# Windowed attention in blocks of 32 queries by 64 keys: scores and value products as 64x32 tiles of the TensorE array

## The chip, the cores and the metric

The kernel runs on one core of a Trainium2 chip. The metric is device time in microseconds (us): the median of three runs. One further execution was recorded by the profiler; its rows are what the text below quotes. PE is TensorE (matmuls), PEld its weight loads, DVE VectorE, ACT ScalarE, POOL GpSimd, SP the engine that issues most DMAs. PSUM is the memory that matmuls write, in banks of 2 KB a partition.

## The reference

Attention over 8 batches, 8 heads, 576 tokens and head size 64, with a window: the first four heads see the last 32 positions, the other four every fourth of the last 128. Behind it a rank-32 mix along the sequence (U, V) and a feed-forward layer of 512 to 2048 to 512.

```python
scores = scale * np.matmul(q, k.transpose(0, 1, 3, 2))
mask_plain = (rel >= 0) & (rel < window)                       # window 32
mask_dil = (rel >= 0) & (rel < window * dilation) & (rel % dilation == 0)
scores = np.where(masks, scores, -1000000000.0)
attn = np.exp(scores - max);  attn = attn / (sum + 1e-09);  a = attn @ v
x = a.transpose(0, 2, 1, 3).reshape(B, S, H * D)
h = x.transpose(0, 2, 1) @ U @ V
u = x + h.transpose(0, 2, 1)
out = u + np.maximum(u @ w_ch1, 0.0) @ w_ch2
```

## The kernel before

**Layout.** The host permutes the tokens of the dilated heads so that they too see 32 successive rows. A tile is 64 queries of one half of the heads, and it needs 64 + 32 = 96 keys. A group is two such tiles for the four heads of a half, taken as two pairs (u, h); a batch has nine groups, the kernel 72. What a group computes is masked: of 96 keys a query uses 32.

**A step of attention.** `batch_items` makes eleven steps a batch. Step s first issues the products with v of group s-2 (`products`, L386), then the scores of group s (`scores`, L337), then the division by the sum (`weighted`, L393 to L417); the sum is a column of ones in v, so that v has 65 columns a head. `soften` follows in four pieces: DVE adds the mask and takes the maximum in one operation (L347), ACT takes the exponential (L351). `turn` brings the result to keys by queries: for the first 18 groups by four PE transposes (L361), behind them by eight DVE transposes of 32x32 blocks (L371). Steps 0 and 1 of a batch have scores alone, the last two products alone.

**A matmul's place in the array.** The scores have 64 contraction rows and 64 queries, so that four tiles of 64x64 lie in the array of 128x128. The products have 96 rows and 64 queries, two tiles.

**The mix.** `split` cuts x in a high and a low part (ACT L440, DVE or POOL L442), `t_mm` multiplies by U (L473; five parts of the batch, some with 64 rows, two matmuls each), `t_evict` splits the result (L482 to L486), `mix` multiplies by V (L495) and DVE adds it to x (L497). `turn_x` turns x by DVE transposes and DRAM, `transp` by PE (L548); ACT L553 and DVE L554 make its high and low part (uth, utl).

**The layers.** 36 tiles of 128 tokens go in twelve chunks of three. For each of 16 f of a chunk layer 1 is twelve matmuls of 128x384 into a PSUM tile ph (L714: high w by high u, low by high, high by low), ACT writes hh, DVE hl (L720), and layer 2 is nine matmuls of 128x512 (L734). The three acc tiles are added to x at the end (L759).

**What sets the order.** Attention of batch 0 is the prologue. The work of the other batches is cut into a queue with due times in chunks, 1.5 chunks a batch, and `slot()` puts what is due between the matmuls of the layers. From chunk 1 on PE's order is that of the code (`tc.manual_schedule(engines={PE})`, PE_FROM = 1); in the prologue, in chunk 0, and on the other engines a scheduler sets it. In the prologue and chunk 0 the weights are read and split in a high and a low part as well (L194 to L210).

**PSUM.** Eight banks: "acc" with three, "ph" with two, "ps" with three. "ps" is shared by the products and half of the scores (`banks`), the other half of the scores (s), the four transposes (ptp) of batch 1, the U products (t), the V products (m) and the transposed tiles (tp). In batch 0 scores use "acc" and transposes "ph".

## Time and profile before

| | us |
|---|---|
| three runs: median (lowest to highest) | 1002.73 (999.86 to 1003.53) |
| the profiled execution | 1000.64 |
| its span in the trace | 998.9 |
| first layer-1 matmul of chunk 0 / of chunk 1 | 52.49 / 152.30 |
| PE busy | 973.3, 97% |
| mean granted clock of TensorE | 0.998 |

The chain that ended last, by line, starts so:

```profile
PE ph L714 37%; PE acc L734 37%; PE b L386 4%; PE s L337 3%; PE t L473 2%; DMA v<-vv 1%; ACT p L351 1%; ACT sign L195 1%; ACT sign L196 1%; ACT v L194 1%; DMA raw<-w 1%; PE m L495 1%; DVE utl L554 1%; DMA raw<-vt 1%; PE t L462 1%
```

Three quarters of the time are matmuls of the two layers; the attention's own matmuls are 7% of it. A matmul row of the timeline gives start and length in us, the line, output and inputs, the contraction rows by columns held (96*64), the columns streamed (96x65) and the number of records that follow one another (x16); a fp32 matmul has two records. Layer matmuls are one record each. "f32" stands for fp32r as well.

### The profile page before, as it was taken

How to read it: one execution, taken by the hardware profiler on the slowest of the kernel's cores; microseconds unless marked ns; L12 is line 12 of the kernel's file. 1: busy time of each engine (PE TensorE's matmuls, PEld its weight loads, DVE VectorE, ACT ScalarE, POOL GpSimd, SP SyncE). 2: the span in 40 equal slices, each digit the busy share in tenths (PEclk: the TensorE clock that was granted, in tenths of full speed). 3: DMA queues.
4: the chain of work that ended last, by engine and by line, in shares of the span. 5: the costliest groups of instructions: out<-in, count | busy, mean ns of one | idle time of the engine just before them, and what ended most of it. 6: DMA issues, size and time to landing. Idle time of an engine off the chain costs nothing.

```text
span 998.9 us, 17702 instructions
## 1 busy us (share of the span) xinstructions
PE 973.3 (97%) x6696; PEld 834.6 (84%) x6696; DVE 512.7 (51%) x1704; ACT 320.2 (32%) x785; POOL 134.4 (13%) x136
## 2 busy tenths in 40 slices
PE   6899999999999999999999999999999999999998
PEld 4687777888888898888888888888888888899897
DVE  2579887654367435664357634664536743211211
ACT  4699963222224212232123312232222421111110
POOL 1289850011001100011000200001100110000000
PEclk9999999999999999999999999999999999999999
DMA  9678624321224122341223313342222303100000
GB/s 276 186 231 273 216 67 130 101 85 59 73 77 124 47 75 67 93 119 48 75 61 100 94 28 77 95 127 60 70 62 79 100 17 95 44 1 1 32 1 32
DMA packets 74805, 89.78 MB, mean 90 GB/s; under 512 B 8256, under 2 KB 53376, under 8 KB 74720
## 3 DMA queue, kind: packets, MB, share of 16 engines
q1 hardware_dynamic: 74720, 88.65, 30.5%
q8 instruction: 53, 0.87, 0.4%
q14 instruction: 32, 0.26, 0.1%
...
## 4 chain that ended last, share of the span: by engine, by line
PE 85%; ACT 5%; DMA 4%; DVE 3%; issue 1%; POOL 1%; SPq 0%; DVEq 0%; ACTq 0%
PE ph L714 37%; PE acc L734 37%; PE b L386 4%; PE s L337 3%; PE t L473 2%; DMA v<-vv 1%; ACT p L351 1%; ACT sign L195 1%; ACT sign L196 1%; ACT v L194 1%; DMA raw<-w 1%; PE m L495 1%; DVE utl L554 1%; DMA raw<-vt 1%; PE t L462 1%
## 5 line engine op out<-in xcount | busy, mean ns | idle before, releaser
L734 PE MATMUL acc<-w2h,hh 128*128 128x512 f32 x576 | 231.1, 401 | 0.3 <-ACT hh L719 0.3
L734 PE MATMUL acc<-w2h,hl 128*128 128x512 f32 x576 | 225.9, 398 | 4.5 <-DVE hl L720 4.4
L734 PE MATMUL acc<-w2l,hh 128*128 128x512 f32 x576 | 227.0, 394 | 0.0
L720 DVE SCALAR_TENSOR_TENSOR hl<-ph,hh 128x384 fp32r<-128x384 f32 x192 | 106.3, 555 | 234.7 <-ACT hh L719 233.4
L719 ACT ACTIVATE hh<-ph 128x384 fp32r<-128x384 f32 x192 | 93.8, 489 | 404.4 <-PE ph L714 403.8
L714 PE MATMUL ph<-uth,w1h 128*128 128x384 f32 x768 | 169.1, 341 | 0.9 <-ACT uth L553 0.9
L714 PE MATMUL ph<-utl,w1h 128*128 128x384 f32 x768 | 167.3, 338 | 0.8 <-DVE utl L554 0.8
L714 PE MATMUL ph<-uth,w1l 128*128 128x384 f32 x768 | 167.2, 338 | 0.0
L714 PEld LDWEIGHTS ph<-uth,w1h 128*128 128x128 f32 x768 | 136.8, 188 | 16.3 <-ACT uth L553 1.2
L371 DVE STREAM_TRANSPOSE pt<-p 32x128 f32<-32x128 f32 x432 | 130.4, 302 | 27.2 <-ACT p L351 21.7
L351 ACT ACTIVATE p<-p,nmax 128x96 f32<-128x96 f32 x288 | 91.3, 367 | 164.0 <-DVE nmax L347 160.5
L714 PEld LDWEIGHTS ph<-utl,w1h 128*128 128x128 f32 x768 | 134.2, 188 | 3.3 <-DVE utl L554 1.1
L734 PEld LDWEIGHTS acc<-w2h,hl 128*128 128x128 f32 x576 | 107.7, 187 | 34.7 <-DVE hl L720 9.5
L714 PEld LDWEIGHTS ph<-uth,w1l 128*128 128x128 f32 x768 | 134.4, 188 | 2.1 <-issue 0.6
L442 POOL TENSOR_TENSOR xhl<-x,xhl 128x256 fp32r<-128x256 f32 (+1 forms) x65 | 50.3, 781 | 627.0 <-ACT xhl L440 603.3
L734 PEld LDWEIGHTS acc<-w2h,hh 128*128 128x128 f32 x576 | 107.9, 187 | 20.7 <-issue 1.1
L734 PEld LDWEIGHTS acc<-w2l,hh 128*128 128x128 f32 x576 | 108.2, 188 | 15.5
L347 DVE CUSTOM_DVE_ANT_0 p<-s,mask_sb 128x96 f32<-128x96 f32 x162 | 34.6, 253 | 82.3 <-PE b L337 69.3
L386 PEld LDWEIGHTS b<-v,pt 96*64 96x64 f32 x1152 | 41.7, 143 | 21.5 <-issue 18.7
L337 PE MATMUL s<-qk 64*64 64x96 f32 x648 | 47.3, 280 | 8.1 <-DMA qk<-qk 6.5
L497 DVE TENSOR_TENSOR x<-x,m 128x256 f32<-128x256 f32 (+1 forms) x74 | 30.5, 416 | 46.9 <-PE m L495 41.7
L386 PE MATMUL b<-v,pt 96*64 96x65 f32 x1152 | 52.2, 234 | 0.0
...
## 6 DMA issues: line engine op xcount, KB each, us to landing
...
v<-vv SPq DMA_DIRECT2D x126, 97.5 KB, 2.0
...
```

Of the source, the lines that this page charges most:

```text
L337: nc.tensor.matmul(sp[h][i * QB:(i + 1) * QB, u, :], lhsT=q_, rhs=k_, start=True, stop=True, tile_position=(h * D, i * QB))
L347: nc.vector.tensor_tensor_reduce(out=p_sb[:, n], in0=sp[h][:, u], in1=mask_sb[:, mask_kind(*tile_of(g, 0))], scale=-1.0 / 8.0, scalar=3.0e ...
L351: nc.scalar.activation(out=p_sb[:, n], in_=p_sb[:, n], func=AF.Exp, bias=nmax[:, n:n + 1], scale=-1.0,)
L371: nc.vector.transpose(out=pt[ks, :, rs], in_=p_sb[rs, :, ks])
L386: last_pv[g] = nc.tensor.matmul(pv[rows[i]:rows[i] + QB, 2 * u + h, :], lhsT=pt[:, 2 * u + h, QB * i:QB * (i + 1)], rhs=loaded[g, 1, i][:, ...
L442: eng.tensor_tensor(out=xl[rs], in0=x[rs], in1=xh[rs].bitcast(F32), op=ALU.subtract)
L473: nc.tensor.matmul(t_ps[b, c], lhsT=u[rs], rhs=m[rs], start=(i == 0 and k == 0), stop=(i == len(batch_parts(b)) - 1 and k == 1),)
L497: nc.vector.tensor_tensor(out=x, in0=x, in1=mp[rs], op=ALU.add)
L714: nc.tensor.matmul(ph, lhsT=w[:, k, :], rhs=u[:, k, :], start=(n == 0), stop=(n == len(seq) - 1))
L719: nc.scalar.activation(out=hh, in_=ph, func=AF.Relu)
L720: nc.vector.scalar_tensor_tensor(out=hl, in0=ph, scalar=0.0, in1=hh.bitcast(F32), op0=ALU.max, op1=ALU.subtract)
L734: nc.tensor.matmul(acc[i], lhsT=h[:, ss], rhs=w, start=(c > 0 and f == 0 and n == 0), stop=(f == FC - 1 and n == 2))
```

## The change

Queries go in blocks of 32, and each block needs 64 keys. A group of two tiles has four blocks (r) and its scores are 16 matmuls of 64 contraction rows by 32 queries with 64 keys, for eight tiles of the array. The products contract over the 64 keys of a block, again 16 matmuls of 64 rows by 32 queries with 65 columns; the two u lie on the upper and the lower half of the rows. Scores and products of a step write one PSUM tile of two banks ("att", one buffer); the even groups of batch 0 use two "acc" banks instead. "ps" keeps one buffer of its three, for everything else in it. The mask, the maximum, the subtraction and the exponential are done for the whole group: two additions of 128 columns, a maximum, a subtraction over 256 columns, one exponential of 256. A group has two PE transposes of 128x128 in place of four, or sixteen DVE transposes of 32 by 2x32 in place of eight of 32 by 4x32. v is loaded with 128 rows in place of 96, with the overlapping keys twice. Parts of the U products that have 64 rows are brought to 128: POOL clears the other rows. Lines of the layers move to L727, L732 to L733 and L747, of the V products to L508, of the final addition to L772.

```diff
-KB = QB + WIN
+KT = QB + WIN
+KB = 2 * WIN
...
-    psum = ctx.enter_context(tc.tile_pool(name="psum", bufs=3, space=bass.MemoryType.PSUM))
+    psum = ctx.enter_context(tc.tile_pool(name="psum", bufs=1, space=bass.MemoryType.PSUM))
...
-    def banks(name):
-        t = psum.tile([P, UNITS * DV + 2 * KB], F32, tag="ps", name=name)
-        return (t[:, 0:UNITS * DV].rearrange("p (u e) -> p u e", e=DV),
-                t[:, UNITS * DV:].rearrange("p (u k) -> p u k", k=KB))
+    def banks(g):
+        if g >= NGB or g % 2:
+            t = psum.tile([P, 2, 512], F32, tag="att", name=f"att{g}", bufs=1)
+            return [t], [t[:, 0], t[:, 1]]
+        t = [psum.tile([P, 512], F32, tag="acc", name=f"att{g}_{i}", bufs=3) for i in range(2)]
+        return [e.unsqueeze(1) for e in t], t
...
-                for i in range(2):
-                    q_, k_ = q_and_k(g, u, h, i)
-                    nc.tensor.matmul(sp[h][i * QB:(i + 1) * QB, u, :], lhsT=q_, rhs=k_, start=True, stop=True,
-                                     tile_position=(h * D, i * QB))
+                for r in range(BLK):
+                    q_, k_ = q_and_k(g, u, h, r)
+                    nc.tensor.matmul(each[h][r * WIN:(r + 1) * WIN, u * KB:(u + 1) * KB], lhsT=q_, rhs=k_,
+                                     start=True, stop=True, tile_position=(h * D, r * WIN))
...
-        nc.vector.tensor_tensor_reduce(
-            out=p_sb[:, n], in0=sp[h][:, u], in1=mask_sb[:, mask_kind(*tile_of(g, 0))], scale=-1.0 / 8.0, scalar=3.0e38,
-            op0=ALU.add, op1=ALU.min, accum_out=nmax[:, n:n + 1],
-        )
-        nc.scalar.activation(
-            out=p_sb[:, n], in_=p_sb[:, n], func=AF.Exp,
-            bias=nmax[:, n:n + 1], scale=-1.0,
-        )
+                nc.vector.tensor_tensor(out=o, in0=e[:, h, 0:2 * KB].rearrange("p (u k) -> p u k", k=KB),
+                                        in1=m.broadcast_to([P, 2, KB]), op=ALU.add)
+        p4 = p_sb.rearrange("p h u k -> p (h u) k")
+        nc.vector.tensor_reduce(out=top, in_=p4, axis=mybir.AxisListType.X, op=ALU.max)
+        nc.vector.tensor_tensor(out=p4, in0=p4, in1=top.unsqueeze(2).broadcast_to([P, UNITS, KB]), op=ALU.subtract)
+        nc.scalar.activation(out=p4, in_=p4, func=AF.Exp, scale=1.0 / 8.0)
...
-        for r in range(P // WIN):
+        for r in range(BLK):
             rs = slice(WIN * r, WIN * (r + 1))
-            for k in (r % 2, r % 2 + 1):
-                ks = slice(WIN * k, WIN * (k + 1))
-                nc.vector.transpose(out=pt[ks, :, rs], in_=p_sb[rs, :, ks])
+            for u in range(2):
+                for k in range(2):
+                    ks = slice(D * u + WIN * k, D * u + WIN * (k + 1))
+                    nc.vector.transpose(out=pt[ks, :, rs], in_=p_sb[rs, :, u, WIN * k:WIN * (k + 1)])
...
-                for i in range(2):
-                    last_pv[g] = nc.tensor.matmul(pv[rows[i]:rows[i] + QB, 2 * u + h, :], lhsT=pt[:, 2 * u + h, QB * i:QB * (i + 1)],
-                                     rhs=loaded[g, 1, i][:, u, hs], start=True, stop=True)
+                for r in range(BLK):
+                    row = rows[r // 2] + r % 2 * WIN
+                    o = 2 * KB + h * DV
+                    last_pv[g] = nc.tensor.matmul(each[u][row:row + WIN, o:o + DV], lhsT=pt[us_, h, WIN * r:WIN * (r + 1)],
+                                                  rhs=loaded[g, 1, r // 2][us_, r % 2, hs], start=True, stop=True,
+                                                  tile_position=(u * D, row))
...
+        if rs != slice(0, P):
+            rest = slice(0, rs.start) if rs.start else slice(rs.stop, P)
+            nc.gpsimd.memset(xhl[rest].bitcast(F32), 0.0)
...
-                t_ps[b, c], lhsT=u[rs], rhs=m[rs],
+                t_ps[b, c], lhsT=u, rhs=m,
...
-        mp = psum.tile([P, HALF_D], F32, tag="ps", name=f"m{b}_{i}_{c}")
+        mp = psum.tile([P, HALF_D], F32, tag="ps", name=f"m{b}_{i}_{c}", bufs=1)
...
-            tp = psum.tile([P, KC, P], F32, tag="ps", name=f"tp{t}")
+            tp = psum.tile([P, KC, P], F32, tag="ps", name=f"tp{t}", bufs=1)
```

What it moves, in three places. PE, a full step of batch 2's kind in chunk 1, before (the last products of one group, the scores of another, and the layer matmul behind them; b and s are PSUM tiles of "ps"):

```order
L386 MATMUL b_4_2235<-v_0_2148,pt_79 64x65
L386 MATMUL b_4_2235<-v_1_2150,pt_79 64x65
L386 MATMUL b_4_2235<-v_0_2148,pt_79 64x65
L386 MATMUL b_4_2235<-v_1_2150,pt_79 64x65
L337 MATMUL s_2244<-qk_2080 64x96 x2
L337 MATMUL b_4_2235<-qk_2080 64x96 x2
L337 MATMUL s_2244<-qk_2080 64x96 x2
L337 MATMUL b_4_2235<-qk_2080 64x96 x2
L714 MATMUL ph_5_2263<-uth_1919,w1h_86 128x384 x4
```

and the same step after:

```order
L387 MATMUL att_2483<-v_0_2376,pt_79 32x65 x2
L387 MATMUL att_2483<-v_1_2378,pt_79 32x65 x2
L387 MATMUL att_2483<-v_0_2376,pt_79 32x65 x2
L387 MATMUL att_2483<-v_1_2378,pt_79 32x65 x2
L333 MATMUL att_2483<-qk_2302 32x64 x16
L727 MATMUL ph_5_2525<-uth_2107,w1h_84 128x384 x4
```

The step stands where it stood; it has 16 and 16 matmuls in place of 8 and 8, into one tile.

PE, the passage from chunk 0 to chunk 1, before (acc is the last of layer 2, m are V products of batch 1, tp tiles turned by PE, ph the first of layer 1):

```order
L734 MATMUL acc_2_687<-w2h_1537,hl_15_1916 128x512
L495 MATMUL m_3_0_1715<-ts_0_1675,vs 128x256
L495 MATMUL m_4_0_1721<-ts_0_1675,vs 128x256
L337 MATMUL s_1875<-qk_1153 64x96 x4
L337 MATMUL b_0_1874<-qk_1153 64x96 x4
L548 MATMUL tp_1921<-id_sb,x_399 128x128 x4
L548 MATMUL tp_1928<-id_sb,x_389 128x128 x4
L548 MATMUL tp_1952<-id_sb,x_1096 128x128 x4
L714 MATMUL ph_0_1979<-uth_1919,w1h_86 128x384 x4
```

and after, from the third U product on (two more stand ahead of it, behind the last of layer 2):

```order
L486 MATMUL t_0_1790<-xhl_3_0_1809,us 64x256 x2
L486 MATMUL t_0_1790<-xhl_4_0_1840,us 64x256 x2
L508 MATMUL m_0_0_1867<-ts_0_1859,vs 128x256
L508 MATMUL m_1_0_1879<-ts_0_1859,vs 128x256
L508 MATMUL m_2_0_1890<-ts_0_1859,vs 128x256
L508 MATMUL m_3_0_1899<-ts_0_1859,vs 128x256
L508 MATMUL m_4_0_1905<-ts_0_1859,vs 128x256
L561 MATMUL tp_2109<-id_sb,x_461 128x128 x4
L561 MATMUL tp_2116<-id_sb,x_449 128x128 x4
L561 MATMUL tp_2148<-id_sb,x_1248 128x128 x4
L727 MATMUL ph_0_2175<-uth_2107,w1h_84 128x384 x4
```

The U products and the first three V products, which lay among the last layers of chunk 0, stand between the chunks now; the scores have left that place.

DVE, one group in the steady part, before (ssum and xp are the division of an older group, p the softmax, pt its transposes, hl the remainder of layer 1):

```order
L393 TENSOR_SCALAR ssum_4525<-b_2_4503 128x4
L394 RECIPROCAL ssum_4525<-ssum_4525 128x4
L417 TENSOR_TENSOR xp_4528<-b_2_4503,ssum_4525 128x256
L347 ISA p_4521,nmax_4522<-b_2_4503,mask_sb 128x96
L347 ISA nmax_4522 128x1
L347 ISA p_4521,nmax_4522<-b_2_4503,mask_sb 128x96
L347 ISA nmax_4522 128x1
L371 STREAM_TRANSPOSE pt_79<-p_4521 32x4x32 x8
L720 SCALAR_TENSOR_TENSOR hl_2_4550<-ph_2_4532,hh_2_4549 128x384
```

and one after (this group's division writes two x tiles of 64 rows):

```order
L398 TENSOR_SCALAR ssum_4278<-att_4242 128x4
L400 RECIPROCAL ssum_4278<-ssum_4278 128x4
L425 TENSOR_TENSOR x_2734<-att_4242,ssum_4278 64x256
L425 TENSOR_TENSOR x_4152<-att_4242,ssum_4278 64x256
L346 TENSOR_TENSOR p_4275<-att_4242,mask_sb 128x128 x2
L349 TENSOR_REDUCE top_4286<-p_4275 128x4
L350 TENSOR_TENSOR p_4275<-p_4275,top_4286 128x256
L369 STREAM_TRANSPOSE pt_79<-p_4275 32x2x32 x16
L733 SCALAR_TENSOR_TENSOR hl_2_4322<-ph_2_4302,hh_2_4321 128x384
```

Sixteen transposes stand ahead of hl in place of eight, and the softmax ahead of them is four operations of whole groups.

More of the change, by code (lines that the diff above doesn't have):

```diff
@@ L167, in attention_moe_kernel @@
     NPT = 2
-    pts = [const.tile([KB, UNITS, P], F32, name=f"pt{i}") for i in range(NPT)]
-    for p in pts:
-        nc.gpsimd.memset(p, 0.0)
+    pts = [const.tile([P, 2, P], F32, name=f"pt{i}") for i in range(NPT)]
     def fetch64(i):
@@ L333, in scores @@
+    def scores(g, all_, each):
         for u in range(2):
             for h in range(2):
-                for i in range(2):
-                    q_, k_ = q_and_k(g, u, h, i)
-                    nc.tensor.matmul(sp[h][i * QB:(i + 1) * QB, u, :], lhsT=q_, rhs=k_, start=True, stop=True,
-                                     tile_position=(h * D, i * QB))
-        p_sb = work.tile([P, UNITS, KB], F32, tag="p", name=f"p{g}", bufs=2)
-        pool, n_ = (early, 3) if g < NGB else (work, 2)
-        nmax = pool.tile([P, UNITS], F32, tag="nmax", name=f"nmax{g}", bufs=n_)
@@ new lines, in scores, with soften @@
+        state[g] = [work.tile([P, 2, 2, KB], F32, tag="p", name=f"p{g}", bufs=2), all_]
+    def soften(g):
+        p_sb, all_ = state[g]
+        pool, n_ = (early, 3) if g < NGB else (work, 2)
+        top = pool.tile([P, UNITS], F32, tag="top", name=f"top{g}", bufs=n_)
+        m = mask_sb[:, mask_kind(*tile_of(g, 0))].unsqueeze(1)
+        n = 2 // len(all_)
+        for i, e in enumerate(all_):
+            for h in range(n):
+                o = p_sb[:, i * n + h]
+                nc.vector.tensor_tensor(out=o, in0=e[:, h, 0:2 * KB].rearrange("p (u k) -> p u k", k=KB),
[4 more added lines that the diff above has]
+        nc.scalar.activation(out=p4, in_=p4, func=AF.Exp, scale=1.0 / 8.0)
@@ L358, in turn @@
         if g < PE_T:
-            tp = psum.tile([KB, UNITS, P], F32, tag="ph" if g < NGB else "ps", name=f"ptp{g}", bufs=2 if g < NGB else 3)
-            for u in range(UNITS):
-                nc.tensor.transpose(out=tp[:, u, :], in_=p_sb[:, u], identity=id_sb)
+            tp = psum.tile([P, 2, P], F32, tag="ph" if g < NGB else "ps", name=f"ptp{g}", bufs=2 if g < NGB else 1)
+            for h in range(2):
+                nc.tensor.transpose(out=tp[:, h, :], in_=p_sb[:, h].rearrange("p u k -> p (u k)"), identity=id_sb)
             if g in PT_ACT:
@@ L375, in attention_moe_kernel, with products @@
     dil_rows = {}
-    def products(g, pt, pv):
+    def products(g, pt, all_, each):
         b = g // NGB
@@ L458, in t_first @@
             m = xps.pop(i)
[L459 removed]
+        new = not t0_ps
         if new:
[L461 removed]
+            t0_ps.append(psum.tile([2 * RANK, 2, HALF_D], F32, tag="ps", name="t0", bufs=1))
+        t_ps[0, c] = t0_ps[0][:, c]
         nc.tensor.matmul(t_ps[0, c], lhsT=held_u[0][rs, k * RANK:(k + 2) * RANK], rhs=m[rs],
[L463 removed]
+                         start=new, stop=(i == (0 if c else len(DPART) - 2)), skip_group_check=True)
     def t_mm(b, i, c):
```

79 lines of the change are left out of this document (39 added, 40 removed).

## Prediction

> **What bounds the kernel now.** I read the page's busy table first, then the chain of the work that ended last, and then the busy time of each engine in three stretches.
>
> ```profile
> PE 973.3 (97%) x6696; PEld 834.6 (84%) x6696; DVE 512.7 (51%) x1704; ACT 320.2 (32%) x785; POOL 134.4 (13%) x136
> PE 85%; ACT 5%; DMA 4%; DVE 3%; issue 1%; POOL 1%; SPq 0%; DVEq 0%; ACTq 0%
> 0.00:25.00 25.00, 17.41 (x172) 11.52 (x172) 7.21 (x52) 12.15 (x32) 3.15 (x11) 1.00 0.95 276
> 75.00:100.00 25.00, 23.78 (x198) 19.38 (x198) 23.91 (x64) 24.69 (x52) 22.85 (x19) 1.00 0.89 273
> 500.00:600.00 100.00, 100.00 (x738) 86.02 (x737) 57.28 (x214) 28.46 (x75) 7.31 (x10) 1.00 0.25 72
> ```
>
> The stretches give PE, PEld, DVE, ACT and POOL in that order, then the granted clock, the DMA share and GB/s. There are three regimes. Up to 25 us the DMA engines are full (0.95). In chunk 0, here from 75 to 100, ACT (24.69 of 25), DVE (23.91) and POOL (22.85) are nearly full: the weights are being split there, and PE waits for them. From chunk 1 on PE is full and DVE is at 57%. So in the long part a microsecond less on PE is a microsecond less of time, so long as DVE doesn't come late. How near it is to coming late is one row of the waits from 160 to 900 us (sum, count, longest):
>
> ```profile
> PE acc L734 <- DVE hl L720: 3.0, 7, 0.5
> ```
>
> All times are summed against the profiled run, 1000.64 us (span 998.9, so 1.7 lies around it); the median of the three runs shown is 2.1 higher, within their spread.
>
> **Steady state: what an attention step costs PE.** The timeline of PE around one step, then around a step that has scores alone:
>
> ```profile
> 513.50 0.40 PE L734 MATMUL acc<-w2h,hl 128*128 128x512 f32 x1
> 513.83 0.69 PE L386 MATMUL b<-v,pt 96*64 96x65 f32 x16
> 514.45 0.30 PE L337 MATMUL s<-qk 64*64 64x96 f32 x2
> 514.46 0.30 PE L337 MATMUL b<-qk 64*64 64x96 f32 x2
> 514.58 0.25 PE L337 MATMUL s<-qk 64*64 64x96 f32 x2
> ...
> 514.75 0.25 PE L337 MATMUL s<-qk 64*64 64x96 f32 x2
> ...
> 514.94 0.50 PE L734 MATMUL acc<-w2h,hh 128*128 128x512 f32 x1
> 515.27 0.39 PE L734 MATMUL acc<-w2l,hh 128*128 128x512 f32 x1
> 515.50 0.40 PE L734 MATMUL acc<-w2h,hl 128*128 128x512 f32 x1
> ...
> 500.56 0.30 PE L337 MATMUL s<-qk 64*64 64x96 f32 x2
> ...
> 501.05 0.97 PE L714 MATMUL ph<-uth,w1h 128*128 128x384 f32 x4
> 501.86 0.85 PE L714 MATMUL ph<-uth,w1l 128*128 128x384 f32 x4
> 502.55 0.86 PE L714 MATMUL ph<-utl,w1h 128*128 128x384 f32 x4
> ```
>
> Undisturbed, one layer-2 matmul starts 0.23 after the last (515.27 to 515.50) and a layer-1 group of four takes 0.69 (501.86 to 502.55). The step costs what its starts add: 513.50 to 513.83 is 0.10 too long, products take 0.62, scores 0.49, and 514.94 to 515.27 is again 0.10 too long: **1.31 us**. Scores alone cost the same 0.10 + 0.49 (500.56 to 501.05) + 0.12 (501.05 to 501.86 over 0.69), some 0.70; products alone, by the parts of the full step, 0.10 + 0.62 + 0.10 = 0.82. Batches 2 to 7 have 42 full steps, 12 with scores alone, 12 with products alone: 55.0 + 8.4 + 9.8 = 73 us of PE.
>
> Why 0.62 and 0.49: a fp32 matmul is two records (x16 for eight). Records on different tiles of the array start 0.01 apart (514.45 and 514.46, two in each row), so the tiles run beside one another. Scores are 16 records on four tiles, four rounds. From 514.58 to 514.75 are two rounds of 96 columns, so a round is 0.083 and a column 0.86 ns; four rounds are 0.33 and 0.16 is loading and draining. Products are 96 rows high, so two tiles and eight rounds of 65 columns, 8 x 0.056 = 0.45 and 0.17.
>
> After, both shapes are 64x32 tiles, eight in the array, 32 records each: four rounds of 65 columns (0.22) and four of 64 (0.22), with one load and drain for both, since the shape doesn't change between them. With 0.05 for eight starts one after another, that is 0.10 + 0.17 + 0.44 + 0.05 + 0.10 = 0.86. Against it stands the number of instructions. PE's sequencer was seen once between the two lines, and it reached the scores' wait when the products had just begun:
>
> ```profile
> L337 PEldq EVENT_SEMAPHORE  x1: 51/51/51, 513.9 to 513.9; - x1
> ```
>
> So it runs about eight matmuls ahead, and of 32 the other 24 must be supplied while the first run, in some 0.5 us. I add 0.10 to each step for that, an estimate from this row with the bounds 0 and the rate of the densest supply seen (below). A full step is then 0.96, saving 0.35; products alone (one shape, 0.22 in place of 0.44) 0.64, saving 0.18; scores alone 0.64, saving 0.06. 42 x 0.35 + 12 x 0.18 + 12 x 0.06 = 17.6; **PE -17.5** (-22 to -24 without the supply charge; the other end is the second rival).
>
> The U products of 64 rows become 128 rows, with zeros below; their POOL memsets lie on an engine with 7.31 of 100 us busy. By the two shapes' rows, 28 x (306 - 282) ns, **-0.5**.
>
> ```profile
> L473 PE MATMUL t<-xhl,us 128*64 128x256 f32 x112 | 22.4, 282 | 0.8 <-POOL xhl L442 0.8
> L473 PE MATMUL t<-xhl,us 64*64 64x256 f32 x28 | 6.7, 306 | 0.5 <-DVE xhl L442 0.5
> ```
>
> **DVE in the steady state.** These groups give busy sum, mean ns, and idle before:
>
> ```profile
> L371 DVE STREAM_TRANSPOSE pt<-p 32x128 f32<-32x128 f32 x432 | 130.4, 302 | 27.2 <-ACT p L351 21.7
> L524 DVE STREAM_TRANSPOSE z<-x 128x512 f32<-128x512 f32 x30 | 21.3, 711 | 16.8 <-DMA zd<-z 16.4
> L347 DVE CUSTOM_DVE_ANT_0 p<-b,mask_sb 128x96 f32<-128x96 f32 x126 | 26.7, 249 | 0.1
> L351 ACT ACTIVATE p<-p,nmax 128x96 f32<-128x96 f32 x288 | 91.3, 367 | 164.0 <-DVE nmax L347 160.5 <-DVE ssum L393 3.3
> ```
>
> Between 302 ns at 128 columns and 711 at 512 lie 1.07 ns a column; a 64-column transpose is then 235 ns, and 16 of them take 3.9 us in place of 8 x 0.31 = 2.5. Softmax is four fused operations of 0.25 now, and two mask additions, a maximum over 256 and a subtraction over 256 after. No row shows the latter two; the nearest is a 256-column addition at 415 ns (L497, below), and with two of 128 columns at some 0.28 it is 1.4 us against 1.0. DVE stays below 80%, so its sum doesn't bind. But the hi/lo remainder of a layer-1 tile (hl) that stands behind the block of transposes comes up to 1.4 to 1.9 us later. Seven times of some 150 (16 a chunk, some 77 us a chunk) it was late already, by at most 0.5, so most have slack. If one in twenty more is late by 1.4, it is 54 groups' blocks x 0.05 x 1.4 = 4; **+4**, between 0 and one block in four at 1.7 (23, the third rival).
>
> The single buffer of "ps": a mix product is followed by the addition that frees it.
>
> ```profile
> 242.64 0.28 PE L495 MATMUL m<-ts,vs 128*128 128x256 f32 x1
> 243.03 0.42 DVE L497 TENSOR_TENSOR x<-x,m 128x256 f32<-128x256 f32 x1 [1.20 <-PE m L495]
> 244.15 0.28 PE L495 MATMUL m<-ts,vs 128*128 128x256 f32 x1
> ```
>
> It is free 0.81 after the start, the next user comes 1.51 after: **0** here, hidden by the layer matmuls between.
>
> **Where that buffer does cost: from chunk 0 to chunk 1.** Before, PE's gap between the last layer-2 work of chunk 0 and the first layer-1 matmul of chunk 1 is this:
>
> ```profile
> 146.98 0.39 PE L495 MATMUL m<-ts,vs 128*128 128x256 f32 x2
> 152.30 0.97 PE L714 MATMUL ph<-uth,w1h 128*128 128x384 f32 x4 [0.94 <-ACT uth L553]
> ...
> L554 DVE TENSOR_TENSOR utl<-tp,uth 128x512 fp32r<-128x512 f32 x6 | 4.1, 685 | 0.3 <-ACT uth L553 0.2
> L553 ACT CAST uth<-tp 128x512 fp32r<-128x512 f32 x6 | 3.3, 580 | 0.0
> L759 DVE TENSOR_TENSOR x<-acc,x 128x512 f32<-128x512 f32 x36 | 24.4, 688 | 6.1 <-PE acc L734 5.9
> ```
>
> 5.3 us. In the new order of PE ten U products, five mixes and three transposed tiles stand in that gap, all through the one buffer, each waiting for its reader: U 1.2 (ten of 256 columns at two thirds of a layer-1 matmul's 0.69 / 4), three operations that split its result 1.2 (256 columns, by the 0.42 of L497), five mixes x 0.85 (0.81 and a restart) = 4.3, three tiles x (0.55 of PE + 0.58 + 0.69) = 5.4, and between them DVE does three final additions of 0.69 = 2.1: 14.2. That is +9, less about 1 of U and mix work that left the chunk; **+8** (5 if the additions fall beside ACT's casts, 12 if DVE has transposes of z ahead of them as well).
>
> **Before chunk 1.** v comes with 128 rows in place of 96, a third more bytes, and the first stage has this chain:
>
> ```profile
> v<-vv SPq DMA_DIRECT2D x126, 97.5 KB, 2.0
> 8.05 7.06 DMA v<-vv
> 15.13 7.86 DMA raw<-vt
> 23.01 0.52 ACT v L194
> 26.42 0.91 PE s L337 x8
> 27.33 1.06 PE b L386 x16
> ```
>
> Nine groups of batch 0 are 66 KB more each, 0.6 MB, at 276 GB/s **+2.2**. Behind it PE's scores (0.91) and products (1.06) go to about half; I let half of that 1.0 a group lie on the path, where DVE isn't the later one: nine times 0.5, -4.5. Together **-2** (-6 if DVE keeps up, +3 if the transfers end last). In chunk 0 ACT is the full engine; it does one Exp of 256 columns a group (estimate 0.52, from 367 ns at 96) for four of 0.27 pitch, 9 x 0.55 = -5; DVE and POOL, both near full there, have the larger softmax and the memsets: +3. **-2** (-7 to +4).
>
> **Sum.** -17.5 - 0.5 + 4 + 8 - 2 - 2 = -10: 1000.64 - 10 = **990**.
>
> **Rivals.** First, slower: the array may carry only as many column streams as today, four records at a time. Nothing in the trace runs more than four, and the pairs at 514.45 are the only evidence of tiles running together. Then products are 8 rounds and scores 8: 0.10 + 0.17 + 0.45 + 0.44 + 0.10 + 0.05 = 1.31, products alone 0.85, scores alone 0.84, +2 on PE. With +4 and +8 and -2, **1012**. It decides from an attention saving below 10 us on.
>
> Second, supply: the densest row has four records in 0.083, 21 ns each. If that is the issue rate and not the array's, 64 records take 1.32, a step 1.6, +0.3 x 42 + 0.3 x 24 = +20; with the rest **1030**. For it: 0.083 is also what 96 columns take at 0.86, so the two can't be told apart there; against it: records start 0.01 apart in pairs.
>
> The Trainium skill, "TensorE: Matmul & The Clock Gate", section "Wait — 56ns, not 53.3ns?", says that starts of matmuls never come closer than about 25 ns however few the columns; by that rule 64 records would take at least 1.6 us a step, and this rival would hold. The trace disagrees as far as it goes: 16 records of scores lie within 0.49, 31 ns each with loading and draining, and the rows 514.45 and 514.46 hold four starts.
>
> Third, it is given back: one block of transposes in four makes hl late by 1.7 (+23 in place of +4), or half that and the boundary at 12: **1001 to 1009**, no change or slower.
>
> **How the numbers follow.** Forecast 0.66 (its own range 976 to 999), first rival 0.13, second 0.05, third 0.16. The range, **976 to 1013**, takes in the first and third and leaves out the second and a tenth of the forecast. A measurement tells about 0.5% from no change, 5 us: faster 0.61 (forecast below 995.6), same 0.16 (its upper end and half the third), slower 0.23.
>
> **What would show it.** The start of L387 to the start of the next layer matmul in a full step: 0.76 if right, 1.1 by the first rival, 1.4 by the second. Waits of layer 2 for hl in 160 to 900: 7 us in place of 3. The gap before chunk 1's first L727: 13 to 14 us in place of 5.3. A 64-column transpose at 235 ns; at 300 the steady stalls would double and the third rival begins.

## The result and the profile after

The changed kernel takes 1013.70 us (median of four runs, 1010.67 to 1015.53) against 1001.56 us (four runs, one more than in the table of the kernel before; 999.86 to 1003.53): a ratio of 1.0118, 95% interval 1.0085 to 1.0151. It is slower by 1.2%, where 990 was forecast; the time lies 0.7 us above the range. The profiled execution has a span of 1013.6 us against 998.9.

The busy time of the engines and the chain by line, on the page of the changed kernel:

```profile
PE 955.7 (94%) x8964; PEld 821.9 (81%) x8964; DVE 623.5 (62%) x1857; ACT 259.5 (26%) x569; POOL 139.5 (14%) x148
PE ph L727 35%; PE acc L747 34%; DVE pt L369 4%; PE att L387 2%; PE att L333 2%; DMA qk<-qk 2%; PE t L486 2%; DVE utl L567 2%; DMA raw<-w 1%; DVE hl L733 1%; DVE v L200 1%; PE m L508 1%; DVE p L350 1%; ACT sign L194 1%; DMA x<-xd 1%
```

PE is busy for 17.6 us less, and attention's two lines have gone from 7% of the chain to 4%. DVE's transposes stand in the chain with 4%, where they weren't named before. So the attention did get cheaper on PE, and the span grew by 14.7 us all the same.

Where it grew is read by cutting PE's time at three points: the first layer-1 matmul of chunk 0, the end of its last layer-2 matmul (counted as 0.23 us behind its start, where the next could begin), and the first layer-1 matmul of chunks 1 and 11. The table has these stretches for all runs (us, from the rows of PE in the one profiled execution of each; time is the median of the runs).

| run | up to chunk 0 | chunk 0 | gap to chunk 1 | chunks 1 to 10 | chunk 11 to its last matmul | time |
|---|---|---|---|---|---|---|
| before | 52.5 | 94.5 | 5.3 | 775.3 | 67.4 | 1001.6 |
| the change | 51.4 | 102.5 | 17.6 | 771.0 | 67.3 | 1013.7 |
| e1 before, one buffer | 58.3 | 93.6 | 16.1 | 779.4 | 67.4 | 1023.3 |
| e2 before, 16 transposes | 51.8 | 95.3 | 5.3 | 778.7 | 67.4 | 1005.7 |
| e3 products in layer 1's buffers | 51.7 | 129.7 | 1.8 | 764.4 | 67.3 | 1021.0 |
| e4 two pieces | 51.3 | 103.2 | 17.6 | 770.3 | 67.3 | 1012.0 |
| e5 fused softmax | 54.4 | 93.1 | 13.7 | 762.7 | 67.3 | 997.3 |
| e6 batch 1 earlier | 50.5 | 115.1 | 3.6 | 768.1 | 67.3 | 1009.2 |
| e7 remainder first | 51.7 | 102.3 | 17.6 | 758.8 | 67.3 | 1003.0 |
| e8 all three | 54.7 | 108.2 | 3.6 | 755.9 | 67.3 | 995.3 |
| e9 fused, remainder first | 54.8 | 93.1 | 13.7 | 757.0 | 67.3 | 991.9 |
| e10 as e9, gap's buffers | 55.1 | 94.2 | 5.5 | 756.8 | 67.3 | 983.6 |
| e11 before, remainder first | 55.5 | 94.2 | 5.5 | 771.6 | 67.4 | 995.9 |
| e12 as e9, tiles' buffers | 54.7 | 93.1 | 4.7 | 755.3 | 67.3 | 981.3 |

For the change the differences are -1.1, +8.0, +12.3, -4.3 and -0.1: a loss of 20 us around the first chunk and a gain of only 4 in ten steady chunks. The first column has to be read with care: e11's edit acts from chunk 2 on, and its execution still reached chunk 0 3.0 us later than that of the kernel before.

**The steady step.** The timeline of PE around a step with scores alone, then around a full step of the changed kernel:

```profile
517.84 0.40 PE L747 MATMUL acc<-w2h,hl 128*128 128x512 f32 x1
518.17 0.45 PE L333 MATMUL att<-qk 64*32 64x64 f32 x32
518.55 0.97 PE L727 MATMUL ph<-uth,w1h 128*128 128x384 f32 x4
...
530.90 0.40 PE L747 MATMUL acc<-w2h,hl 128*128 128x512 f32 x1
531.23 0.46 PE L387 MATMUL att<-v,pt 64*32 64x65 f32 x32
531.50 0.62 PE L333 MATMUL att<-qk 64*32 64x64 f32 x32
532.05 0.50 PE L747 MATMUL acc<-w2h,hh 128*128 128x512 f32 x1
532.39 0.39 PE L747 MATMUL acc<-w2l,hh 128*128 128x512 f32 x1
```

From the products to the next layer matmul is 0.82 us. The forecast was to be known by 0.76 there, the first two rivals by 1.1 and 1.4. With 0.10 on each side the step costs 1.02, down from 1.31. The 32 records of the products make way within 0.27 (531.23 to 531.50), where four records at a time would have taken eight rounds of 0.056, 0.45: the eight tiles run together.

Against this stand the waits of PE from 160 to 900 us (sum, times, longest). Before, there was one row with 3.0 us; now there are more, and these are the largest:

```profile
PE acc L747 <- DVE hl L733: 12.8, 12, 2.2
PE tp L561 <- DVE utl L567: 3.6, 2, 2.2
PE m L508 <- DVE x L510: 2.6, 5, 0.6
```

The last two stand mostly in the gap ahead of chunk 1. The long ones of the first row stand at the ends of chunks, but for one of 1.65 at 180.34; DVE's timeline at one of them:

```profile
398.83 0.49 DVE L346 TENSOR_TENSOR p<-att,mask_sb 128x128 f32<-128x128 f32 x2
399.35 0.42 DVE L349 TENSOR_REDUCE top<-p 128x4 f32<-128x256 f32 x1
399.81 0.42 DVE L350 TENSOR_TENSOR p<-p,top 128x256 f32<-128x256 f32 x1
400.72 3.98 DVE L369 STREAM_TRANSPOSE pt<-p 32x64 f32<-32x64 f32 x16 [0.48 <-ACT p L351]
404.73 1.90 DVE L567 TENSOR_TENSOR utl<-xt,uth 128x512 fp32r<-128x512 f32 x3
406.55 0.55 DVE L733 SCALAR_TENSOR_TENSOR hl<-ph,hh 128x384 fp32r<-128x384 f32 x1
```

A whole group's softmax, 0.48 of waiting for the one exponential, 16 transposes and the three low parts of the next chunk's tokens stand ahead of the hl of f = 15, the last of the chunk. PE waits 2.17 us for it.

**The gap.** PE's timeline between chunk 0 and chunk 1:

```profile
153.19 0.87 PE L747 MATMUL acc<-w2h,hl 128*128 128x512 f32 x3
154.75 1.39 PE L486 MATMUL t<-xhl,us 128*64 128x256 f32 x10 [0.69 <-DVE x L510]
158.40 0.58 PE L508 MATMUL m<-ts,vs 128*128 128x256 f32 x1 [2.26 <-ACT ts L499]
159.50 0.58 PE L508 MATMUL m<-ts,vs 128*128 128x256 f32 x1 [0.52 <-DVE x L510]
...
163.88 1.11 PE L561 MATMUL tp<-id_sb,x 128*128 128x128 f32 x4 [0.51 <-DVE x L510]
167.16 1.11 PE L561 MATMUL tp<-id_sb,x 128*128 128x128 f32 x4 [2.17 <-DVE utl L567]
169.68 1.12 PE L561 MATMUL tp<-id_sb,x 128*128 128x128 f32 x4 [1.40 <-DVE utl L567]
171.47 1.65 PE L727 MATMUL ph<-uth,w1h 128*128 128x384 f32 x4 [0.68 <-ACT uth L566]
```

From the first V product on, each waits until the reader of the one before is done with the buffer. The matmuls last 0.58 where the same shape took 0.28, and the first group of layer 1 takes 1.65 for 0.97: the granted clock is halved, as the busy table by stretch says (PE, PEld, DVE, ACT, POOL, then the clock):

```profile
160.00:171.00 11.00, 5.16 (x16) 3.00 (x15) 4.94 (x9) 1.34 (x3) 0.00 (x0) 0.50 0.28 73
300.00:400.00 100.00, 98.33 (x944) 85.38 (x943) 66.45 (x213) 20.29 (x47) 7.77 (x11) 1.00 0.30 84
408.00:411.00 3.00, 3.00 (x10) 2.44 (x8) 1.76 (x3) 0.00 (x0) 0.00 (x0) 0.50 0.43 160
```

The last row is the stretch behind the stall at 404.98 to 407.15: three microseconds at half clock, though PE was full in them. The middle one holds a stall of 1.31 us (it ended at 329.64) and keeps the full clock.

**Chunk 0.** The waits of PE and of ACT from 50 to 150 us that are new or have grown (before, the first was 1.1, once, and ACT waited for the maxima 5.2, once, at 149.5 and so behind chunk 0):

```profile
PE ptp L358 <- ACT p L351: 5.4, 4, 2.1
PE m L508 <- DVE x L510: 3.5, 2, 2.1
ACT p L351 <- DVE p L350: 9.4, 7, 2.5
```

ACT, which prepares the weights there, waits 9.4 us for the subtraction of the softmax, and PE's transposes wait for ACT. The busy table from 75 to 100 us, in the order used above:

```profile
75.00:100.00 25.00, 19.42 (x197) 16.88 (x198) 23.68 (x43) 20.14 (x36) 21.42 (x17) 0.80 0.77 251
```

Before, in the same stretch, ACT was busy for 24.69 and PE for 23.78, at a clock of 1.00. DVE and POOL are nearly as full as they were; ACT isn't full any more, PE is busy for 4.4 us less, and its clock was 0.80.

### The profile page after: what moved, and what is told of

Its sections match the earlier page's. It is cut to its first block, busy times and chain, and to the rows that moved or that the text cites. A ratio compares the mean times of both kernels' runs of the same rounds, so it can differ in the third digit from the quotient of the medians.

```text
span 1013.6 us, 22097 instructions
## 1 busy us (share of the span) xinstructions
PE 955.7 (94%) x8964; PEld 821.9 (81%) x8964; DVE 623.5 (62%) x1857; ACT 259.5 (26%) x569; POOL 139.5 (14%) x148
## 4 chain that ended last, share of the span: by engine, by line
PE 76%; DVE 12%; DMA 4%; ACT 4%; issue 2%; SPq 1%; DVEq 0%; ACTq 0%
PE ph L727 35%; PE acc L747 34%; DVE pt L369 4%; PE att L387 2%; PE att L333 2%; DMA qk<-qk 2%; PE t L486 2%; DVE utl L567 2%; DMA raw<-w 1%; DVE hl L733 1%; DVE v L200 1%; PE m L508 1%; DVE p L350 1%; ACT sign L194 1%; DMA x<-xd 1%
## 5 line engine op out<-in xcount | busy, mean ns | idle before, releaser
L747 PE MATMUL acc<-w2h,hl 128*128 128x512 f32 x576 | 230.2, 401 | 13.3 <-DVE hl L733 13.2
L733 DVE SCALAR_TENSOR_TENSOR hl<-ph,hh 128x384 fp32r<-128x384 f32 x192 | 106.3, 554 | 207.5 <-ACT hh L732 205.6
L747 PE MATMUL acc<-w2h,hh 128*128 128x512 f32 x576 | 232.1, 403 | 0.7 <-ACT hh L732 0.7
L747 PE MATMUL acc<-w2l,hh 128*128 128x512 f32 x576 | 228.8, 397 | 0.0
L369 DVE STREAM_TRANSPOSE pt<-p 32x64 f32<-32x64 f32 x864 | 203.9, 236 | 27.3 <-ACT p L351 15.9
L732 ACT ACTIVATE hh<-ph 128x384 fp32r<-128x384 f32 x192 | 93.8, 488 | 471.7 <-PE ph L727 467.7
L727 PE MATMUL ph<-uth,w1h 128*128 128x384 f32 x768 | 170.8, 344 | 0.7 <-ACT uth L566 0.7
L727 PE MATMUL ph<-uth,w1l 128*128 128x384 f32 x768 | 169.4, 342 | 0.0
L727 PE MATMUL ph<-utl,w1h 128*128 128x384 f32 x768 | 168.6, 341 | 0.0
L727 PEld LDWEIGHTS ph<-uth,w1h 128*128 128x128 f32 x768 | 139.3, 191 | 16.3 <-ACT uth L566 1.3
L747 PEld LDWEIGHTS acc<-w2h,hl 128*128 128x128 f32 x576 | 108.7, 189 | 46.3 <-DVE hl L733 20.7
L727 PEld LDWEIGHTS ph<-uth,w1l 128*128 128x128 f32 x768 | 137.2, 191 | 1.1 <-issue 0.3
L727 PEld LDWEIGHTS ph<-utl,w1h 128*128 128x128 f32 x768 | 136.0, 190 | 1.4
L747 PEld LDWEIGHTS acc<-w2h,hh 128*128 128x128 f32 x576 | 108.9, 189 | 19.4 <-ACT hh L732 1.0
L747 PEld LDWEIGHTS acc<-w2l,hh 128*128 128x128 f32 x576 | 109.0, 189 | 15.5
L351 ACT ACTIVATE p<-p 128x256 f32<-128x256 f32 x72 | 30.0, 416 | 101.2 <-DVE p L350 101.1
L387 PEld LDWEIGHTS att<-v,pt 64*32 64x32 f32 x2304 | 22.7, 110 | 34.7 <-issue 20.6
L333 PE MATMUL att<-qk 64*32 64x64 f32 x2304 | 44.0, 237 | 6.1 <-DMA qk<-qk 6.1
L201 POOL TENSOR_TENSOR v<-v,sign 128x512 int32<-128x512 int32 (+1 forms) x34 | 45.2, 1329 | 32.8 <-DVE v L200 20.0
L453 ACT CAST xhl<-x 128x256 fp32r<-128x256 f32 (+1 forms) x70 | 27.7, 403 | 76.1 <-DVE x L425 33.7
```

The costliest lines, as they stand in the source:

```text
L201: nc.gpsimd.tensor_tensor(out=vi, in0=vi, in1=s32, op=ALU.add)
L333: nc.tensor.matmul(each[h][r * WIN:(r + 1) * WIN, u * KB:(u + 1) * KB], lhsT=q_, rhs=k_, start=True, stop=True, tile_position=(h * D, r * ...
L351: nc.scalar.activation(out=p4, in_=p4, func=AF.Exp, scale=1.0 / 8.0)
L369: nc.vector.transpose(out=pt[ks, :, rs], in_=p_sb[rs, :, u, WIN * k:WIN * (k + 1)])
L387: last_pv[g] = nc.tensor.matmul(each[u][row:row + WIN, o:o + DV], lhsT=pt[us_, h, WIN * r:WIN * (r + 1)], rhs=loaded[g, 1, r // 2][us_, r ...
L453: nc.scalar.copy(out=xh[rs], in_=x[rs])
```

## The experiments

**e1, one buffer in the kernel before.** Only the allocation of PSUM is changed.

```diff
-        tp = psum.tile([P, KC, P], F32, tag="ps", name=f"tp{t}")
+        tp = psum.tile([P, KC, P], F32, tag="one", name=f"tp{t}", bufs=1)
```

and so for the U and V products and batch 1's transposes of p (each a line of its own, left out here); "ps" keeps two buffers for products and scores.

> The kernel before with one PSUM buffer for the U and V products, the transposed tiles and the transposes of p, and two for products and scores; nothing else changed. Theory: the single buffer makes the passage from chunk 0 to chunk 1 long, because the U and V products of batch 1 then stand between the chunks in PE's order. The gap there goes from 5.3 us to 14 to 17, the granted clock falls to 0.5 in it, and the kernel to 1010 to 1015 us. If the waits of the V products inside chunk 0 come from it as well, chunk 0 (94.7 us) grows by 3 to 5. Rival: the long gap comes from the full-height U products or from the longer DVE work of the change; then the gap stays under 8 us and the time within 1000 to 1005. The steady chunks keep their length under both (750 us from the start of chunk 1 to the start of chunk 11 to within 2).

Measured: 1023.27 us, ratio 1.0221 (1.0185 to 1.0257), above the 1010 to 1015 expected. Its PE timeline in the gap:

```profile
152.00 1.53 PE L473 MATMUL t<-xhl,us 64*64 64x256 f32 x10
155.20 0.39 PE L495 MATMUL m<-ts,vs 128*128 128x256 f32 x1 [1.67 <-ACT ts L486]
...
160.47 1.11 PE L548 MATMUL tp<-id_sb,x 128*128 128x128 f32 x4 [0.52 <-DVE x L497]
...
168.06 1.65 PE L714 MATMUL ph<-uth,w1h 128*128 128x384 f32 x4 [0.68 <-ACT uth L553]
```

The kernel before now has nearly the same gap, 16.1 us, with the clock halved: the buffer alone makes it. Chunk 0 does not grow (93.6), so its 8 us come from elsewhere. That the time is even above the changed kernel's has two further parts. PE reaches chunk 0 5.8 us later; in batch 0 the two halves of the U products take turns in the one buffer here and share a tile in the change, but that this is the reason was not tested, and 3 us of it are within what e11 shows. And the steady chunks take 4.1 more, where no more than 2 was expected; the steps with V products account for 2.9 of that.

**e2, sixteen transposes in the kernel before.**

```diff
-                nc.vector.transpose(out=pt[ks, :, rs], in_=p_sb[rs, :, ks])
+                for n in (slice(0, 2), slice(2, 4)):
+                    nc.vector.transpose(out=pt[ks, n, rs], in_=p_sb[rs, n, ks])
```

> The kernel before with each DVE transpose of 32 by 4x32 issued as two of 32 by 2x32: 16 a group for 8, about 3.9 us for 2.5. Theory: the block of transposes, followed by the three low parts of the next chunk, makes the remainder of the last layer-1 tiles of a chunk late; the waits of layer 2 for hl in 160 to 900 us go from 3.0 us in total to 8 to 12, with single ones near 2 us, the granted clock falls to 0.5 for some 3 us behind the long ones, and the kernel takes 1008 to 1013 us. Rival: the late remainders come from the order in which DVE's work stands, moved by the new softmax; then these waits stay under 5 us and the time under 1004.

Measured: 1005.65 us, 1.0041 (1.0028 to 1.0053). The wait for hl from 160 to 900 us:

```profile
PE acc L735 <- DVE hl L721: 4.8, 7, 0.9
```

The waits are 4.8 us for 3.0 before, under the 5 of the rival and not the 8 to 12 of the theory, and the longest is 0.9; the time lies between the two forecasts (1004 and 1008). More transposes alone do not make the long stalls. That the wider softmax ahead of them is the other part is tested in e5.

**e3, the products in layer 1's buffers.** The U and V products of the second half of batch 1 and the tp of chunk 1 get tag "ph"; one of the three lines:

```diff
+        mp = (psum.tile([P, HALF_D], F32, tag="ph", name=f"m{b}_{i}_{c}", bufs=2) if (b, c) == (1, 0) else
```

> The changed kernel with the second half of batch 1's U and V products and the transposed tiles of chunk 1 in the two buffers that layer 1 uses, the single buffer left to the rest. PE's order then has these products among the last layers of chunk 0 again. Theory: the gap falls from 17.4 us to about 5 or 6 with the clock at 1.00, and the kernel from 1013.7 to 1000 to 1003. If the single buffer also makes chunk 0 long, its 102.6 us fall by 3 or more and the time is 996 to 1000. Rival: what left the gap stands in chunk 0 and takes as long there: time above 1008.

Measured: 1021.01 us, 1.0191 (1.0174 to 1.0207). The gap is 1.8, but chunk 0 takes 129.7: the rival. By the code, a U product that gathers five parts holds one of the two buffers of layer 1 while it waits; how much of the 27 us this is was not separated. The largest of PE's waits in chunk 0 (48 to 160 us) and two others, for which the change has 0.5 and nothing:

```profile
PE ptp L358 <- ACT p L351: 8.2, 5, 2.7
...
PE ptp L358 <- ACT ts L500: 5.3, 1, 5.3
PE t L487 <- POOL xhl L455: 4.7, 5, 3.1
```

**e4, transposes in two pieces.**

```diff
-            timed += ... + [(i + POST_AT, step[-1])]
+            timed += ... + [(i + at_, lambda part=part, f=step[-1]: f(part=part)) for part, at_ in enumerate((0.7, 1.2))]
```

> The changed kernel with the 16 DVE transposes of a group issued in two pieces of eight, half a step apart (batches 2 to 7). Theory: a remainder of layer 1 now stands at most 2 us behind a piece, so the waits of layer 2 for hl in 160 to 900 us fall from 12.8 to under 5, the stretches at half clock behind them go, and the time falls by 6 to 11 to 1003 to 1008. Rival: it is DVE's total that makes it late (624 us busy, and the same here): waits above 10 and time within 1011 to 1016.

Measured: 1011.97 us, 1.0108 (1.0087 to 1.013), and the waits for hl are nearly as they were (12.8):

```profile
PE acc L749 <- DVE hl L735: 11.8, 12, 2.2
```

Both figures are those of the rival, but the run separates less than was meant. DVE's timeline at the stall still has sixteen transposes in a row from 400.61 to 404.59 with the three utl behind them, since a scheduler orders DVE. The pieces were never apart, so nothing follows from it on DVE's total.

**e5, the fused softmax.**

```diff
-                nc.vector.tensor_tensor(out=o, in0=e[:, h, 0:2 * KB]..., in1=m.broadcast_to([P, 2, KB]), op=ALU.add)
-        nc.vector.tensor_reduce(out=top, in_=p4, axis=mybir.AxisListType.X, op=ALU.max)
-        nc.vector.tensor_tensor(out=p4, in0=p4, in1=top..., op=ALU.subtract)
-        nc.scalar.activation(out=p4, in_=p4, func=AF.Exp, scale=1.0 / 8.0)
+                for u in range(2):
...
+                    nc.vector.tensor_tensor_reduce(
+                        out=o, in0=e[:, h, u * KB:(u + 1) * KB], in1=m, scale=-1.0 / 8.0, scalar=3.0e38,
+                        op0=ALU.add, op1=ALU.min, accum_out=nmax[:, w:w + 1])
+                    nc.scalar.activation(out=o, in_=o, func=AF.Exp, bias=nmax[:, w:w + 1], scale=-1.0)
```

> The changed kernel with the softmax of before: four operations of mask and maximum in one, of 64 columns each, and four exponentials, for the two additions, maximum, subtraction and one exponential. Theory: chunk 0 (102.5 us, 94.5 before) is long because ACT's one exponential waits for the whole chain on DVE, PE's transposes of p wait for it, and the weights behind it on ACT wait as well; with the fused form chunk 0 takes 94 to 97 us, the waits of PE's transposes for the exponential fall from 5.4 us to under 2, and the late remainders at the chunks' ends get about 1 us earlier (waits for hl in 160 to 900 from 12.8 to 6 to 9). Time 1000 to 1006. Rival: chunk 0 is long by the waits of V products for their addition or by DVE's total; then it stays over 100 and the time over 1009.

Measured: 997.34 us, ratio to the kernel before 0.9962 (0.9952 to 0.9972), 16 us under the changed kernel. Chunk 0 is back at 93.1, and the waits of PE for ptp and of ACT for p are gone from the lists of waits there. The steady chunks gain 8.3 as well (waits for hl 8.3 us, longest 1.4), and the gap 3.9: PE's ten U products now stand ahead of the last layer-2 matmuls (at 143.53). No other single edit to the changed kernel brings as much. The fused form also has a price: all five runs with it reach chunk 0 at 54.4 to 55.1 us, the others of the changed kernel at 50.5 to 51.7. So the wide softmax, of which the prediction expected a gain on ACT in chunk 0, does gain some 3 us ahead of it.

**e6, batch 1 due earlier.**

```diff
-HI1 = 0.85
+HI1 = 0.7
```

> The changed kernel with one number changed: the work of batch 1 is due by 0.70 of chunk 0, not 0.85 (HI1). PE's order then has the last U products ahead of f = 13 and the V products among the layers 13 to 15. Theory: the gap between the chunks falls from 17.6 us to 5 to 8 with the clock at 1.00, chunk 0 grows by 2 to 4 for the products that it has to carry, and the time falls by 6 to 11, to 1003 to 1008. Rival: as in the run that gave these products layer 1's buffers, they wait in chunk 0 for as long as they did between the chunks: chunk 0 over 112 us and time over 1010.

Measured: 1009.19 us, 1.0084 (1.0065 to 1.0104). The gap is 3.6, chunk 0 115.1: of 14.0 us 12.7 reappear there. Its waits for ptp alone are 7.9 us. Time between both forecasts; the stretches follow the rival. Moved to chunk 0, the chain waits there for nearly as long.

**e7, the last remainder first.**

```diff
-        nc.vector.tensor_tensor(out=l, in0=tp, in1=h.bitcast(F32), op=ALU.subtract)
+        with tc.issue_after(last_hl[0].ins) if c > 1 else ExitStack():
+            nc.vector.tensor_tensor(out=l, in0=tp, in1=h.bitcast(F32), op=ALU.subtract)
...
+            last_hl[0] = nc.vector.scalar_tensor_tensor(out=hl, in0=ph, scalar=0.0, in1=hh.bitcast(F32),
```

> The changed kernel with the three low parts of a chunk's tokens (utl) put behind the remainder of the last layer-1 tile (hl of f = 15) on DVE, from chunk 2 on. Theory: the long waits are a block of softmax and 16 transposes with three utl ahead of that remainder; with the utl behind it, the waits of layer 2 for hl in 160 to 900 fall from 12.8 us to under 5, no stretch at half clock follows a chunk's end, and the steady part from the start of chunk 1 to the start of chunk 11 falls from 771.0 by 6 to 11. Rival: the utl are then late for layer 1 of the next chunk and the wait goes over to it: the steady part stays within 768 to 773.

Measured: 1003.04 us, 1.0024 (1.0013 to 1.0034); the steady chunks take 758.8, 12.2 less, a little more than expected. DVE's timeline at the same place, and PE's wait for hl from 160 to 900 us:

```profile
398.94 3.98 DVE L369 STREAM_TRANSPOSE pt<-p 32x64 f32<-32x64 f32 x16 [0.48 <-ACT p L351]
402.96 0.56 DVE L736 SCALAR_TENSOR_TENSOR hl<-ph,hh 128x384 fp32r<-128x384 f32 x1
403.43 1.89 DVE L568 TENSOR_TENSOR utl<-xt,uth 128x512 fp32r<-128x512 f32 x3
```

```profile
PE acc L750 <- DVE hl L736: 2.4, 3, 1.7
```

The same transposes, 3.98 us long, now cost nothing at this place: it was the order behind them. A little of the rival is there too: PE's V products now wait 3.5 us for the split results of the U products (ACT ts), which they didn't in the change, and the intervals with V products cost 3.8 us more.

**e8, e5 to e7 together.**

> The three edits together: fused softmax, batch 1 due by 0.70, remainder first. Theory: they act in different places (chunk 0, the gap, the chunks' ends), so their gains add up: chunk 0 at 95 to 99 us, gap 5 to 8, steady part 760 to 765, time 986 to 995, below the kernel before. Rival: chunk 0 is bound by the preparation of the weights and takes back what the products cost there: time 997 to 1004.

Measured: 995.31 us, 0.9943 (0.9925 to 0.996). The time is 0.3 above the theory's range, and the stretches don't follow it. Chunk 0 takes 108.2, not 95 to 99; with its gap of 3.6 that is 111.8 against 106.8 with the fused softmax alone, so the rival's mechanism holds for the earlier due time. The steady part (755.9) is shorter than the 760 to 765 expected, but the two gains don't add up to it: 8.3 and 12.2 off 771.0 would be 750.5. Both take away waits for the same hl.

**e9, e5 and e7 without the earlier due time.**

> The changed kernel with the fused softmax and the remainder first, batch 1 due as in the change (0.85). Theory: what the earlier due time saved in the gap it gave back in chunk 0 and more, since there batch 1's work waits for the same engines; without it the start of chunk 1 is at 161 us, as with the fused softmax alone, the steady part at 754 to 758, and the time 988 to 992. Rival: the run of all three is slower for another reason than the due time: 994 to 997.

Measured: 991.92 us, 0.991 (0.9895 to 0.9925), steady part 757.0, start of chunk 1 at 161.6: as the theory had it.

**e10 and e12, the gap's buffers on top of e9.** e12 gives the transposed tiles of chunk 1 the two buffers of layer 1; e10 also gives the V products of the gap the three of layer 2.

```diff
-            tp = psum.tile([P, KC, P], F32, tag="ps", name=f"tp{t}", bufs=1)
+            tp = (psum.tile([P, KC, P], F32, tag="ph", name=f"tp{t}", bufs=2) if c == 1 else
+                  psum.tile([P, KC, P], F32, tag="ps", name=f"tp{t}", bufs=1))
```

> As the run with fused softmax and remainder first, and in the passage from chunk 0 to chunk 1 the transposed tiles use layer 1's two buffers and the second half of batch 1's V products the three of layer 2, in place of the one buffer. Theory: the gap of 13.7 us is a chain through one buffer; it falls to 7 to 9, the half clock in it to less than 3 us, and the time by 5 to 7 to 982 to 987. Rival: the chain is bound by DVE's and ACT's operations and not by the buffer: gap over 11, time over 987.

> As the run before last, but with only the transposed tiles in layer 1's buffers; the V products stay in the one buffer. Theory: of the 13.7 us some 3 are waits of the transposed tiles for the low part before them, so the gap is 10 to 11 us and the time 985 to 989. Rival: the V products in the one buffer end later than the tiles in any case, and nothing is gained: gap over 13.

Measured: e10 983.61 us, 0.9828 (0.9813 to 0.9842); e12 981.30 us, 0.9803 (0.9788 to 0.9818). The gap falls to 5.5 and 4.7 us, further than either expectation; e10's time is in its range, e12's is 3.7 us below. So the tiles' buffers are enough, and the three for the V products bring nothing on top. PE's timeline of e12 says why:

```profile
148.39 0.38 PE L507 MATMUL m<-ts,vs 128*128 128x256 f32 x1 [0.40 <-ACT ts L498]
150.00 0.39 PE L507 MATMUL m<-ts,vs 128*128 128x256 f32 x1 [1.23 <-DVE x L509]
150.22 0.60 PE L561 MATMUL tp<-id_sb,x 128*128 128x128 f32 x4
150.90 0.39 PE L507 MATMUL m<-ts,vs 128*128 128x256 f32 x1
151.12 0.60 PE L561 MATMUL tp<-id_sb,x 128*128 128x128 f32 x4
151.80 0.38 PE L507 MATMUL m<-ts,vs 128*128 128x256 f32 x1
152.49 1.62 PE L730 MATMUL ph<-uth,w1h 128*128 128x384 f32 x4 [0.31 <-DVE utl L568]
```

With another buffer two of the tiles go between the V products, each in the time in which the other's reader works; the first tile lies in chunk 0 (142.51), and the last V product in chunk 1 (155.77). The U products stand ahead of the layer 2 of f = 15, as in e9. The V products last 0.38 again: the clock stays full. e12 is the fastest kernel of the study, 2.0% under the one before and 3.2% under the changed one by the medians.

**e11, the last remainder first in the kernel before.**

> The kernel before with the remainder of the last layer-1 tile put ahead of the three low parts (from chunk 2 on). Theory: its waits for hl are 3.0 us in all and none is long enough for the clock to fall, so the steady part of 775.3 falls by 2 to 5 only and the time to 996 to 1000. Rival: the order costs the kernel before as much as the changed one: 8 or more.

The edit is that of e7. Measured: 995.90 us, 0.9947 (0.993 to 0.9963), steady part 771.6, 3.7 less, as the theory had it. So the better order is worth 4 us to the kernel before and 12 to the changed one. Between e11 and e12, which have the same order there, the steady part differs by 16.3 us. By the intervals between layer matmuls from chunk 1 on, the attention steps give 16.3 and the U products 2.9; the V products take back 0.4, and 2.3 go to intervals with nothing in them, since e12 still has 3.3 us of waits for hl and e11 none.

## Why the prediction was wrong

**PE's steps: right, a little too large.** This adds what lies between starts of layer matmuls beyond their undisturbed 0.233 and 0.174 us, from chunk 1 to the end: full steps 50.4 before and 38.2 after, products alone 8.5 and 5.8, scores alone 6.4 and 6.1. That is 15.2 where the sum had 17.5. The full step is what came out dearer, 1.02 for 0.96: behind the products, the 32 records of the scores take 0.55 us (531.50 to 532.05), and alone 0.38 (518.17 to 518.55). If the difference of 0.17 is the supply of instructions, the 0.10 charged for it was too small; no run tests that it is. The U products at full height brought 2.8 (17.0 to 14.2), for which 0.5 stood; which part of the edit brought the rest was not tested. The first two rivals are out. (The first one's 1012 is also a slip: its own terms, with all of the sum's others, give 1010.)

**DVE in the steady part: +12.8, not +4.** This is the first mis-sized term. The intervals between layer matmuls with nothing in them are too long by 17.4 us in sum before and by 30.2 after. Of the 12.8, 9.8 are waits for hl (12.8 against 3.0), and what is left fits two stretches of 3 us at half clock. The third rival had the mechanism and put it anywhere in the chunk, one block in four. The duration was right (a 64-column transpose takes 236 ns, as worked out). What was missed is the place: the prediction looked at one hl behind one block of transposes and found slack, where at a chunk's end the three utl stand between them, and the whole line is late by their sum. And the two longest stalls, of 2.17 us, are paid again by the clock. e7 takes out 12.2 us by order alone, e5 8.3 by an earlier end of the block, both together 14.0 (e9), and e2 shows that sixteen transposes cost the kernel before only 3.4.

**The gap: +12.3, not +8.** The mechanism stood in the prediction, and e1 shows it in the kernel before. The size: from the end of chunk 0 to the first V product it took 4.5 for 2.4, the five V products 1.09 each for 0.85, the three tiles 7.6 us (163.88 to 171.47) for 5.4. In the last two it is mostly half clock, which the sum had left out. The first V product came 2.26 after the U products, for 1.2: ACT's first operation of the split ended at 156.53, and DVE's began only at 157.17, behind the three final additions. These had 2.1 in the sum and held the chain up by no more than that 0.64, which hides a part of the miss.

**Chunk 0: +8.0, not -2.** The step that failed outright: "ACT is the full engine; it does one Exp of 256 columns a group ... for four of 0.27 pitch, 9 x 0.55 = -5". ACT's sum did fall (its exponentials from 50 to 150 us took 12.3 us before and 3.8 after), but the time went into waiting. One exponential for the group can begin only when mask, maximum and subtraction have gone through DVE for all 256 columns, and ACT's work on the weights stands behind it. Two rows of the changed kernel's groups by shape, from 50 to 150 us and from 200 to 900:

```profile
L350 DVE TENSOR_TENSOR p<-p,top 128x256 f32<-128x256 f32 x9 | 7.9, 876 | 0.1
...
L350 DVE TENSOR_TENSOR p<-p,top 128x256 f32<-128x256 f32 x50 | 22.1, 442 | 1.6
```

The subtraction takes twice its time there, where POOL is at 21 to 24 of 25 us up to 125; its only price in the prediction is the 415 ns of a steady row, and in chunk 0 the whole softmax and the memsets were put at +3 without a row. It isn't long everywhere: three of the nine take 410 to 424 ns, and the six that begin beside an operation of POOL take 815 to 1504. One of these, and the exponential behind it:

```profile
83.85 1.27 POOL L208 TENSOR_TENSOR w1l<-v,w1h 128x512 fp32r<-128x512 f32 x1 [1.08 <-issue]
84.10 1.30 DVE L350 TENSOR_TENSOR p<-p,top 128x256 f32<-128x256 f32 x1
85.44 0.42 ACT L351 ACTIVATE p<-p 128x256 f32<-128x256 f32 x1 [2.51 <-DVE p L350]
```

Six of ACT's seven waits for p, 8.5 of the 9.4 us, stand behind these six. e5 brings chunk 0 back to 93.1: the softmax is the cause. On DVE it takes 8.8 us from 50 to 150 there (36 fused operations and the reading of their maxima) and 15.9 in the change (4.3 of additions, 3.7 of maxima, 7.9 of subtractions); 4.1 of the difference are what the six subtractions have over 424 ns. How much of the 9 us in chunk 0 is this and how much the lost overlap of four exponentials with four maxima was not separated, nor what part the lower clock has.

**Prologue: -1.1 for -2.** Nothing follows from it: e11 differs from the kernel before by 3.0 there without an edit to it.

In all, the steady part was off by 9.7 us (-4.3 for -14), chunk 0 by 10.0, the gap by 4.3 and the prologue by 0.9: together 25, from the forecast's -10 to the +14.7 of the spans. The third rival had two of the sizes in its milder form, half of 23 and 12 at the boundary: 12.8 and 12.3 were measured. That chunk 0 was +8.0 and not -2 is what carried the time past its 1001 to 1009.
